# Query blocks two at a time from DRAM, and five and four exponential buffers instead of four and three, in a pre-LayerNorm attention and gated MLP block

## The chip, the cores and the metric

One core of a Trainium2 chip runs the whole kernel in one launch. The metric is the device time of one execution in microseconds. Timed runs and a separately profiled execution are told apart throughout: durations of single instructions come from the profiled one.

## The reference

A transformer block on 2048 rows of 640 columns: attention with 32 heads of 20 columns each, then a gated product of two matrices of 1728 columns, both behind a layer normalisation without weights, both added to their input.

```
h  = x + A(_layernorm(x), A_wqkv, A_wo)
h2 = h + B(_layernorm(h), B_w_gate, B_w_up, B_w_down)

A: q, k, v = split(x @ wqkv)              # 32 heads of 20
   p = softmax(q k^T * 20 ** -0.5)
   return (p v) @ wo
B: return ((x @ w_gate) * (x @ w_up)) @ w_down
```

Inputs and output are bfloat16, x is 1 x 2048 x 640.

## The kernel before

**Layout.** The 32 heads stand in 8 groups of four. Within a group each head has a slot of 32 partitions, of which 20 hold its query or key columns and one a constant. Rows of queries come in four blocks of 512 (blocks 0 to 3), keys in 16 tiles of 128.

**Stages.** The attention is a stream of 679 stages. Stage i issues score products (line 737, emit_S) for three (even i) or two (odd i) units into the PSUM tile sc0 or sc1, a unit being 128 keys against up to 512 queries of one head. ScalarE then takes one exponential over the whole tile (line 745) and writes it to a buffer E: E0 of 1536 columns for even stages, E1 of 1024 for odd ones. EB = (4, 3) says how many buffers there are of each. In most odd stages and some even ones a further unit goes to VectorE, which makes its exponential from integer operations (di, dm, dt; lines 757 and 640 to 645).

**Attention products.** The products of E with the values (line 885, emit_AV) read E and add up in one PSUM bank. One round is up to four products of different heads, in the four column groups of the array. An E buffer is free when all rounds that read it have been issued.

**The planner.** The order of all instructions is made in Python while the kernel is built. It keeps clocks for TensorE, VectorE and ScalarE (estimates) and, between the scores of one stage and the next, fills TensorE with attention rounds and with pieces of jobs from a queue (fill_step): projections, output products, the MLP's products. Before stage i writes its buffer, free_of(("e", i - 2 * EB[i % 2])) sees to it that the buffer's earlier readers have been issued. Where they haven't, it issues rounds at once, the last of them also with fewer than four heads. Where there is nothing to fill with, idle products are issued (idle_products).

**Queries and keys.** Most projections are written to DRAM in a dense form (dense, line 377) and read back into slots (read_slots, line 400) by four transfers, one per slot. Keys have one tile kT for all 2048 rows. Queries have qa for blocks 0 to 2 and qb for block 3. Groups 0 to 3 of block 0 are made directly in slots, and job spill (line 1130) writes them to DRAM, where a second version of the attention, for sums out of range, would read them. The rows of the slots that transfers never touch are filled once at the start (line 200).

**Tails.** When the queries of a block (block 0) or of half a block (blocks 1 to 3) are normalised, a tail is queued: output product, layer normalisation, MLP (job_glu, job_y), store. The MLP's up and gate matrices come in seven pairs of 256 columns (fp 0 to 6; the last is narrower), 320 KB a matrix. Two buffers for each of up (wu) and gate (wg) are refilled in turn (load_w). When block 3's stages begin, load_res takes the space of qa (wres) for pairs RES0 = 3 to 6, which the tails behind it find there. The last half-tail (last_tail) starts with the kept pairs, then takes 0 and 1, and pair 2 from two E0 buffers.

**Queues.** All transfers are issued by SyncE, one queue in the program's order: a transfer that waits holds those behind it.

Of the kernel before, what the change touches and what calls it, by code (L numbers as in the profile page):

```python
# [10 lines left out]
BF16 = mybir.dt.bfloat16  # L11
# [7 lines left out]
P = 128  # L19
S = 2048  # L20
D = 640
H = 32
DH = 20
NT = S // P
KT = D // P
# [24 lines left out]
SPLIT_3 = 2  # L50
QA = 3 * QB
RES0 = 3
SM_SCALE = float(DH) ** -0.5
# [28 lines left out]
SLACK = 100  # L82
EB = (4, 3)
POOL_LN = 3500
# [4 lines left out]
def kernel(  # L89
# [51 lines left out]
    qa, qb, kT = [[x[:, g, :] for g in range(NG)] for x in (qa_all, qb_all, kT_all)]  # L141
    dense = [dram.tile([D, S], BF16, name=f"dense{m}", bufs=1) for m in range(2)]
# [39 lines left out]
    for m in (1, 0):  # L182
        src = pads[m]
        runs = [(kT_all, 0, GP, QB, S), (kT_all, GP, NG, 0, S)] if m else [(qa_all, 0, GP, QB, QA), (qa_all, GP, NG, 0, QA), (qb_all, 0, NG, 0, QB)]
# [178 lines left out]
    def job_dense(m, t, ch):  # L363
        yield ROUND * KT
        ps = bank()
        for c in range(KT):
            for k in range(0, P, SLOT):
                col = t * P + k
                nc.tensor.matmul(ps[k:k + SLOT, :], lhsT=wqk_half(c, col // HALF)[:, m, col % HALF:col % HALF + SLOT],  # L369
                                 rhs=lnT[:, c, ch * QB:(ch + 1) * QB], start=(c == 0), stop=(c == KT - 1))  # L370
            mm(ROUND)
            if c < KT - 1:
                yield None
        dn = dnp.tile([P, QB], BF16, name="dn")
        nc.vector.tensor_copy(dn[:], ps[:])
        ev(QB, held["slot"])
        nc.sync.dma_start(dense[m][t * P:(t + 1) * P, ch * QB:(ch + 1) * QB], dn[:])
        written[m, t, ch] = clk["dve"] + WRITE
        for it in slot_sets:
            if it["m"] == m and it["ch"] == ch and all((m, x, ch) in written for x in it["ts"]) and not it["on"]:  # L380
                later(3, lambda it=it: read_slots(it))
# [10 lines left out]
    def read_slots(it):  # L392
        if it["on"]:
            return
        it["on"] = True
        m, ch, (g0, g1) = it["m"], it["ch"], it["gs"]
        dst, c0 = (kT_all, ch * QB) if m else (qb_all, 0) if ch == NB - 1 else (qa_all, ch * QB)
        src = dense[m][:, ch * QB:(ch + 1) * QB].rearrange("(g j e) n -> j e g n", j=HPG, e=DH)
        for j in range(HPG):
            nc.sync.dma_start(dst[SLOT * j:SLOT * j + DH, g0:g1, c0:c0 + QB], src[j, :, g0:g1, :])  # L400
        for key in it["keys"]:
            done.add(key)
            ready[key] = max([clk["pe"]] + [written[m, t, ch] for t in it["ts"]]) + READ

    def ensure_qk(key):
        if key not in done and key in slot_of:
            it = slot_of[key]
            for t in it["ts"]:
                ensure(("dn", it["m"], t, it["ch"]))
            read_slots(it)  # L410
        ensure(key)
        clk["pe"] = max(clk["pe"], ready.get(key, 0))
# [60 lines left out]
    LAST_B, LAST_T = NB - 1, [2, 3]  # L473
    first_b = [next(k for k, u in enumerate(us) if all(PASS[segs[v[0]][0]][0] == LAST_B for v in us[k:])) for us in (a_units, d_units)]
    pos = {"a": 0, "d": 0}
# [652 lines left out]
    def spill(j):  # L1128
        src = dense[0][:, 0:QB].rearrange("(g j e) n -> j e g n", j=HPG, e=DH)
        nc.sync.dma_start(src[j, :, 0:G1, :], qa_all[SLOT * j:SLOT * j + DH, 0:G1, 0:QB])  # L1130

# [102 lines left out]
    def load_res():  # L1234
        old = qkp.tile([P, NG, QA], BF16, name="wres", tag="qa")
        for k, fp in enumerate(range(RES0, FP)):
            late["res"][fp] = [w_tile(src, fp, old[:, 2 * k + m, :])
                               for m, src in enumerate((B_w_up, B_w_gate))]

# [133 lines left out]
    def last_tail():  # L1373
# [101 lines left out]

    seen = {"t": 0, "last": False}
    i = 0
    clk["dve"] = max(clk["dve"], clk["pe"])
    while pos["a"] < len(a_units) or pos["d"] < len(d_units):
        now["i"] = i  # L1480
        emit_S(i)
        if i == 0:
            first_rest()
        if not seen["last"] and pos["a"] >= first_b[0] and pos["d"] >= first_b[1]:
            for j in range(HPG):
                ensure(("spill", j))
            load_res()
            seen["last"] = True
        dve_fill(clk["pe"] + AHEAD)
# [119 lines left out]
```

## Time and profile before

| | us |
|---|---|
| timed runs, median of three | 870.62 (863.52 to 872.59) |
| profiled execution, whole | 861.78 |
| its span, first to last instruction | 860.0 |
| first exponential starts | 14.45 |
| last exponential ends | 810.42 |
| granted TensorE clock, mean | 0.999 of full speed |

The page splits the span by engine and by line. PE is TensorE's products, PEld its weight loads, DVE VectorE, ACT ScalarE, POOL GpSimd, SPq SyncE's queue. A row of a group has the line, engine, operation, what it writes and reads, and the count; then busy time, the mean of one in ns, and the engine's idle time just ahead of it with what ended that.

### The profile page before, as it was taken

How to read it: one execution, taken by the hardware profiler on the slowest of the kernel's cores; microseconds unless marked ns; L12 is line 12 of the kernel's file. 1: busy time of each engine (PE TensorE's matmuls, PEld its weight loads, DVE VectorE, ACT ScalarE, POOL GpSimd, SP SyncE). 2: the span in 40 equal slices, each digit the busy share in tenths (PEclk: the TensorE clock that was granted, in tenths of full speed). 3: DMA queues.
4: the chain of work that ended last, by engine and by line, in shares of the span. 5: the costliest groups of instructions: out<-in, count | busy, mean ns of one | idle time of the engine just before them, and what ended most of it. 6: DMA issues, size and time to landing. Idle time of an engine off the chain costs nothing.

```text
span 860.0 us, 34381 instructions
## 1 busy us (share of the span) xinstructions
PE 820.1 (95%) x15264; PEld 406.0 (47%) x15264; DVE 701.9 (82%) x1384; ACT 798.8 (93%) x711; POOL 191.3 (22%) x259
## 2 busy tenths in 40 slices
PE   8999999999999999999999999999999999999996
PEld 6334343332334334455444555555454556555775
DVE  7766788889779989888888889888988888889742
ACT  7999999999999999999999999999999999999621
POOL 2220000445214223212240323121411141114000
PEclk9999999999999999999999999999999999999999
DMA  6211201443330323101314031413510311031310
GB/s 187 70 50 45 68 16 61 105 119 70 66 95 16 118 76 78 40 15 34 100 41 130 24 100 34 116 39 107 124 40 15 107 32 33 9 100 47 88 46 19
DMA packets 94159, 57.62 MB, mean 67 GB/s; under 512 B 24436, under 2 KB 91892, under 8 KB 94004
## 3 DMA queue, kind: packets, MB, share of 16 engines
q1 hardware_dynamic: 94004, 55.36, 24.1%
q8 instruction: 121, 1.98, 0.9%
q14 instruction: 34, 0.28, 0.1%
HBM read 46.94 MB, written 8.16 MB: 64 GB/s over the span
## 4 chain that ended last, share of the span: by engine, by line
PE 49%; DVE 22%; ACT 21%; issue 5%; DMA 1%; POOL 1%; SPq 0%; DVEq 0%; ACTq 0%; POOLq 0%
ACT E L745 21%; PE sc L737 12%; PE acc L885 10%; PE mi L295 9%; PE mi L1251 8%; DVE di L757 7%; DVE di L645 3%; PE mi L369 3%; DVE dm L640 2%; DVE dt L642 2%; PE f L295 2%; PE f L1251 2%; DVE st L220 1%; PE mi L737 1%; DVE hh L1283 1%
## 5 line engine op out<-in xcount | busy, mean ns | idle before, releaser
L745 ACT ACTIVATE E<-sc 128x1536 bf16<-128x1536 f32 (+1 forms) x679 | 781.6, 1263 | 15.6 <-PE mi L737 7.0
L757 DVE TENSOR_SCALAR di<-mi 128x512 int16<-128x512 f32 x350 | 237.7, 684 | 62.1 <-PE mi L737 59.4
L885 PE MATMUL acc<-E,vx 128*32 128x256 bf16 (+1 forms) x2532 | 223.2, 314 | 1.6 <-DVE asb L915 1.4
L737 PE MATMUL sc<-qa,kT 21*128 21x256 bf16 (+1 forms) x1800 | 204.6, 319 | 12.2 <-ACT E L745 9.8
L782 POOL TENSOR_TENSOR rr<-rr,powers 128x8 f32<-128x8 f32 (+1 forms) x44 | 96.5, 2194 | 406.3 <-DMA rr<-sums 406.2
L737 PEld LDWEIGHTS <-kT 21*128 21x128 bf16 x3072 | 85.8, 91 | 212.3 <-issue 201.4
L885 PEld LDWEIGHTS <-vx 128*32 128x32 bf16 x3612 | 81.7, 95 | 106.4 <-issue 99.2
L645 DVE TENSOR_TENSOR di<-di,dm 128x1024 bf16<-128x1024 bf16 x175 | 122.6, 700 | 4.6
L737 PE MATMUL mi<-qa,kT 21*128 21x256 bf16 (+1 forms) x376 | 98.1, 311 | 2.9 <-DVE di L757 1.8
L640 DVE TENSOR_SCALAR dm<-di 128x1024 int16<-128x1024 int16 x175 | 77.2, 441 | 3.5
L885 PE MATMUL acc<-di,vx 128*32 128x256 bf16 (+1 forms) x540 | 76.6, 308 | 0.8 <-DVE di L645 0.5
L642 DVE TENSOR_SCALAR dt<-di 128x1024 int16<-128x1024 int16 x175 | 77.4, 442 | 0.0
L885 PE MATMUL acc<-dt,vx 128*32 128x256 bf16 (+1 forms) x540 | 77.1, 310 | 0.0
L737 PE MATMUL sc<-qb,kT 21*128 21x256 bf16 (+1 forms) x732 | 66.8, 288 | 2.9 <-ACT E L745 2.4
L295 PE MATMUL mi<-wd,hh 128*32 128x320 bf16 x1344 | 62.2, 300 | 1.0 <-DVE di L757 0.6
L1251 PE MATMUL mi<-ln2T,wg 128*32 128x256 bf16 (+1 forms) x1170 | 55.6, 298 | 1.4 <-DVE di L757 0.6
L1251 PE MATMUL mi<-ln2T,wu 128*32 128x256 bf16 (+1 forms) x1170 | 54.6, 298 | 1.2 <-DVE di L757 0.5
L295 PEld LDWEIGHTS <-hh 128*32 128x32 bf16 (+1 forms) x1456 | 45.6, 96 | 17.9 <-issue 8.1
L1251 PEld LDWEIGHTS <-wu 128*32 128x32 bf16 (+1 forms) x1190 | 32.4, 96 | 13.8 <-issue 9.6
L1251 PEld LDWEIGHTS <-wg 128*32 128x32 bf16 (+1 forms) x1190 | 32.6, 96 | 13.2 <-issue 9.2
L295 PE MATMUL mi<-kT,ident 128*32 128x512 bf16 x516 | 36.2, 382 | 1.3 <-DVE di L757 1.0
L266 DVE CAST u<-mi 128x512 bf16<-128x512 f32 x49 | 33.4, 683 | 4.8 <-PE mi L1251 4.8
(139 smaller groups left out, 788.4 us busy)
## 6 DMA issues: line engine op xcount, KB each, us to landing
wu<-in_B_w_up_dram SPq DMA_DIRECT2D x29, 320.0 KB
wg<-in_B_w_gate_dram SPq DMA_DIRECT2D x29, 320.0 KB
dense<-dn SPq DMA_DIRECT2D x36, 128.0 KB
bc<-scr SPq DMA_DIRECT2D x64, 64.0 KB
bc<-scr SPq DMA_DIRECT2D x112, 32.0 KB
xr<-in_A_x_dram SPq DMA_DIRECT2D x16, 160.0 KB
out_dram<-xr SPq DMA_DIRECT2D x14, 160.0 KB
wd<-in_B_w_down_dram SPq DMA_DIRECT2D x13, 160.0 KB
```

Source lines behind the costliest of these rows:

```text
L266: nc.vector.tensor_copy(dst, src)
L295: nc.tensor.matmul(out[k:k + w, :], lhsT=lhsT[:, k:k + w], rhs=rhs, **flags)
L369: nc.tensor.matmul(ps[k:k + SLOT, :], lhsT=wqk_half(c, col // HALF)[:, m, col % HALF:col % HALF + SLOT], rhs=lnT[:, c, ch * QB:(ch + 1) * ...
L640: nc.vector.tensor_scalar(m16[:, 0:n], s16, M_MASK, M_BITS, ALU.bitwise_and, ALU.bitwise_or)
L642: nc.vector.tensor_scalar(t16[:, 0:n], s16, E_MASK, E_BITS, ALU.bitwise_and, ALU.bitwise_or)
L645: nc.vector.tensor_tensor(sb[:, 0:n], sb[:, 0:n], mb[:, 0:n], ALU.mult)
L737: nc.tensor.matmul(dst[:, h * w:(h + 1) * w], lhsT=kT[g][SLOT * j:SLOT * j + VS, (kt + h) * P:(kt + h + 1) * P], rhs=q_of(g, b, c0, w)[SLO ...
L745: nc.scalar.activation(e[:, 0:n], sc[:, 0:n], ACT.Exp, bias=EXP_BIAS, scale=SM_SCALE)
L757: nc.vector.tensor_scalar(t[:, k * BANK:(k + 1) * BANK], sd[:], EXP_A, 0.0, ALU.mult, ALU.max)
L782: nc.gpsimd.tensor_tensor(ri, r16, powers[:, 1:2].to_broadcast([P, n]), ALU.pow)
L885: nc.tensor.matmul(acc["t"][SLOT * j:SLOT * (j + 1), 0:w], lhsT=vx[kt][:, VS * h:VS * h + SLOT], rhs=e, start=(j not in acc["new"]), stop= ...
L1251: nc.tensor.matmul(ps[r0 + x:r0 + x + d, col:col + n], lhsT=wt[:, c, f0 + x:f0 + x + d], rhs=st["ln2T"][:, c, c0:c0 + n], start=(c == 0), ...
```

## The change

The tile qa of three blocks and qb of one become two tiles q0 and q1 of one block each, used in turn. Blocks 0 and 1 are read as before. Block 2 is asked for when block 1's stages begin and all four spills and its dense pieces have been issued, block 3 when block 2's begin (next_q). The memory that this leaves goes to a fifth E0 and a fourth E1 buffer and to a tile of three places (spare) for weights. load_res keeps pairs 4 to 6 instead of 3 to 6: three matrices in spare, three in q0. The last half-tail brings pairs 2 and 3 into four E0 buffers.

```diff
-QA = 3 * QB
-RES0 = 3
+RES0 = 4
-EB = (4, 3)
+EB = (5, 4)
-    qa_all = qkp.tile([P, NG, QA], BF16, name="qa")
-    qb_all = qkp.tile([P, NG, QB], BF16, name="qb")
+    q_all = [qkp.tile([P, NG, QB], BF16, name=f"q{k}") for k in range(2)]
+    spare = qkp.tile([P, 3, KT * FPW], BF16, name="spare")
-        runs = [...] if m else [(qa_all, 0, GP, QB, QA), (qa_all, GP, NG, 0, QA), (qb_all, 0, NG, 0, QB)]
+        runs = [...] if m else [(q_all[0], GP, NG, 0, QB), (q_all[1], 0, NG, 0, QB)]
-        return qb[g][:, c0:c0 + w] if b == NB - 1 else qa[g][:, b * QB + c0:b * QB + c0 + w]
+        return q_all[b % 2][:, g, c0:c0 + w]
-            if it["m"] == m and it["ch"] == ch and all(...) and not it["on"]:
+            if it["m"] == m and it["ch"] == ch and all(...) and not it["on"] and (m or ch < 2):
+    def spilled():
+        for j in range(HPG):
+            ensure(("spill", j))
+    def next_q(b):
+        it = slot_of["q", b, 0]
+        if not all((0, t, b) in written for t in it["ts"]) or not all(("spill", j) in done for j in range(HPG)):
+            later(1, lambda: next_q(b))
+        elif not it["on"]:
+            read_slots(it)
...
     def load_res():
-        old = qkp.tile([P, NG, QA], BF16, name="wres", tag="qa")
+        old = qkp.tile([P, NG * QB], BF16, name="wres", tag="q0")
+        places = [spare[:, k, :] for k in range(3)] + [old[:, k * n:(k + 1) * n] for k in range(3)]
...
-        st["w", 2] = [w_tile(src, 2, e_tile(0)) for src in (B_w_up, B_w_gate)]
+        for fp in range(2, RES0):
+            st["w", fp] = [w_tile(src, fp, e_tile(0)) for src in (B_w_up, B_w_gate)]
...
-            for j in range(HPG):
-                ensure(("spill", j))
-            load_res()
+            if seen["block"] < LAST_B:
+                next_q(seen["block"] + 1)
+            else:
+                load_res()
```

ScalarE's order stays as it is, row for row. TensorE's has the same number of products, in another order. On TensorE before, ahead of the scores of stage 239 (sc_6157 is that stage's PSUM tile; L332 is fill work, a transposition):

```order
L332 MATMUL mi<-ident,ln_6059 128x128
L885 LDWEIGHTS vx_126
L885 MATMUL acc<-E_6009,vx_126 32x512
L885 LDWEIGHTS vx_128
L885 MATMUL acc<-E_6101,vx_128 32x512
L885 LDWEIGHTS vx_128
L885 MATMUL acc<-E_6101,vx_128 32x512
L737 LDWEIGHTS kT
L737 MATMUL sc_6157<-qa,kT 128x512
```

After, ahead of the scores of the same stage (sc_6097):

```order
L750 MATMUL mi<-q_114,kT 128x512
L898 LDWEIGHTS vx_132
L898 MATMUL acc<-dt,vx_132 32x512
L898 LDWEIGHTS vx_134
L898 MATMUL acc<-dt,vx_134 32x512
L898 LDWEIGHTS vx_126
L898 MATMUL acc<-E_5934,vx_126 32x512
L898 LDWEIGHTS vx_128
L898 MATMUL acc<-E_6033,vx_128 32x512
L750 LDWEIGHTS kT
L750 MATMUL sc_6097<-q_114,kT 128x512
```

Before, a round of three heads, with the buffer E_6009 that stage 239 needs, is the last thing ahead of the scores; after, it is a round of four.

On SyncE before, where block 3's stages begin (wres are the kept matrices, wu and wg the streamed ones):

```order
L793 DMA bc_14953<-scr 32x256 x4
L1224 DMA wres<-in_B_w_up_dram 128x5x256
L1224 DMA wres<-in_B_w_gate_dram 128x5x256
L1224 DMA wres<-in_B_w_up_dram 128x5x256
L1224 DMA wres<-in_B_w_gate_dram 128x5x256
L1224 DMA wres<-in_B_w_up_dram 128x5x256
L1224 DMA wres<-in_B_w_gate_dram 128x5x256
L1224 DMA wres<-in_B_w_up_dram 128x5x192
L1224 DMA wres<-in_B_w_gate_dram 128x5x192
L787 DMA scr<-rr 128x8
```

And after:

```order
L1237 DMA spare<-in_B_w_up_dram 128x5x256
L1237 DMA spare<-in_B_w_gate_dram 128x5x256
L1237 DMA spare<-in_B_w_up_dram 128x5x256
L1237 DMA wres<-in_B_w_gate_dram 128x5x256
L1237 DMA wres<-in_B_w_up_dram 128x5x192
L1237 DMA wres<-in_B_w_gate_dram 128x5x192
L800 DMA scr<-rr 128x8
L806 DMA bc_15180<-scr 32x256 x4
L1237 DMA wu<-in_B_w_up_dram 128x5x256
L1237 DMA wg<-in_B_w_gate_dram 128x5x256
L1237 DMA wu<-in_B_w_up_dram 128x5x256
L1237 DMA wg<-in_B_w_gate_dram 128x5x256
```

Eight kept matrices became six, and behind the next normalisation step two streamed pairs follow where there was one.

More of the change, by code (lines that the diff above doesn't have):

```diff
@@ L379, in job_dense @@
         for it in slot_sets:
-            if it["m"] == m and it["ch"] == ch and all((m, x, ch) in written for x in it["ts"]) and not it["on"]:
+            if it["m"] == m and it["ch"] == ch and all((m, x, ch) in written for x in it["ts"]) and not it["on"] and (m or ch < 2):
                 later(3, lambda it=it: read_slots(it))
@@ L409, in ensure_qk @@
                 ensure(("dn", it["m"], t, it["ch"]))
+            if key[0] == "q" and key[1] == 2:
+                spilled()
             read_slots(it)
@@ L473 @@
     LAST_B, LAST_T = NB - 1, [2, 3]
-    first_b = [next(k for k, u in enumerate(us) if all(PASS[segs[v[0]][0]][0] == LAST_B for v in us[k:])) for us in (a_units, d_units)]
+    first_of = [[next(k for k, u in enumerate(us) if all(PASS[segs[v[0]][0]][0] >= b for v in us[k:])) for us in (a_units, d_units)] for b in range(NB)]
+    first_b = first_of[LAST_B]
     pos = {"a": 0, "d": 0}
@@ L1474, in idle_products @@
             mm(ROUND)
-    seen = {"t": 0, "last": False}
+    seen = {"t": 0, "block": 0}
     i = 0
```

16 lines of the change are left out of this document (8 added, 8 removed).

## The prediction

> **What bounds the kernel now.** I read the page first, then the waits, then ScalarE's and TensorE's timelines around the waits, and last the end of the span. In the page, columns of a group's row are busy us, mean ns of one, and the idle time just ahead with what ended it.
>
> ```profile
> span 860.0 us, 34381 instructions
> PE 820.1 (95%) x15264; PEld 406.0 (47%) x15264; DVE 701.9 (82%) x1384; ACT 798.8 (93%) x711; POOL 191.3 (22%) x259
> ...
> PE 49%; DVE 22%; ACT 21%; issue 5%; DMA 1%; POOL 1%; SPq 0%; DVEq 0%; ACTq 0%; POOLq 0%
> ...
> L745 ACT ACTIVATE E<-sc 128x1536 bf16<-128x1536 f32 (+1 forms) x679 | 781.6, 1263 | 15.6 <-PE mi L737 7.0
> ```
>
> Two engines run almost through: TensorE and ScalarE. DMA is 1% of the chain that ended last. ScalarE's 679 exponentials (one per stage) are a stream that is hardly ever idle. The view of waits shows how the two hold each other up (total us, times, longest):
>
> ```profile
> PE sc L737 <- ACT E L745: 12.2, 48, 0.7
> ACT E L745 <- PE mi L737: 7.0, 21, 0.7
> ACT E L745 <- PE sc L737: 5.6, 16, 1.2
> ```
>
> TensorE waits 12.2 us for ScalarE, ScalarE 12.6 us for TensorE's scores. Neither is slack for the other: the kernel is a handshake between two nearly full engines. The stream itself, from ScalarE's timeline (start, length, what, how many, idle before) and the group by shape:
>
> ```profile
> 14.45 22.13 ACT L745 ACTIVATE E<-sc 128x1536 bf16<-128x1536 f32 x19 [1.21 <-PE sc L737]
> ...
> 99.33 30.99 ACT L745 ACTIVATE E<-sc 128x1536 bf16<-128x1536 f32 x27
> ...
> 796.27 14.15 ACT L745 ACTIVATE E<-sc 128x1024 bf16<-128x1024 f32 x12 [0.16 <-PE mi L737]
> ...
> L745 ACT ACTIVATE E<-sc 128x1536 bf16<-128x1536 f32 x340 | 501.5, 1475 | 5.1 <-PE sc L737 3.3 <-PE mi L737 1.1
> ```
>
> It runs from 14.45 to 796.27 + 14.15 = 810.42 us: 795.97 us for 339.5 pairs of a wide and a narrow exponential, 2.345 us a pair. Where it is well fed, 27 of them (14 wide, 13 narrow) take 30.99 us; less one wide of 1.475 that is (30.99 - 1.475) / 13 = 2.270 a pair. So the stream is 339.5 x 0.075 = 25 us longer than it would be if it were fed like that throughout. 12.6 us of it are the visible waits; the rest are exponentials that start late enough to lose their overlap with the one ahead. ScalarE's work is untouched by the change (the same exponentials in the same order), so no more than about 25 us can be won in the stream, and only what late scores cost.
>
> **The change part by part.** *More exponential buffers.* Before the scores of stage i are issued, the planner asks that the buffer of that stage is free (free_of); if it isn't, it places rounds of attention products (L885) there and then, ahead of the scores, even with fewer than four heads in a round. With 4 and 3 buffers this happens in stage 239 and in stage 461. TensorE's and ScalarE's timeline at the two:
>
> ```profile
> 290.36 0.40 PE L885 MATMUL acc<-E,vx 128*32 128x512 bf16 x3
> 290.68 0.60 PE L737 MATMUL sc<-qa,kT 21*128 21x512 bf16 x5
> 291.17 2.37 ACT L745 ACTIVATE E<-sc 128x1024 bf16<-128x1024 f32 x2 [0.67 <-PE sc L737]
> ```
> ```profile
> 550.98 0.95 PE L1251 MATMUL mi<-ln2T,wg 128*32 128x256 bf16 x28
> 551.74 0.27 PE L885 MATMUL acc<-E,vx 128*32 128x256 bf16 x1
> ...
> 552.09 0.27 PE L885 MATMUL acc<-E,vx 128*32 128x256 bf16 x1
> ...
> 552.30 0.28 PE L737 MATMUL sc<-qa,kT 21*128 21x256 bf16 x2
> ...
> 552.79 2.37 ACT L745 ACTIVATE E<-sc 128x1024 bf16<-128x1024 f32 x2 [0.72 <-PE mi L737]
> ```
>
> In the first a round of three heads stands between the fill work and the scores, in the second four rounds do, and ScalarE is idle 0.67 and 0.72 us. To count them I ran the planner of both files and noted each stage in which a buffer had to be freed first: 83 of 679 before, 26 after. Then I matched the 679 exponentials of the trace in turn with the stages and took, for each, how much later it ended than the usual 1.343 (wide) or 0.916 us (narrow) after the one ahead. The 83 stages are late by 10.2 us together, 0.123 each; the other 595 (the first has none ahead) by 18.5 us, 0.031 each. What a forced round costs is the difference, 0.092 us, so 7.6 us in all. 57 such stages go: 57 x 0.092 = **-5.2 us**. From below, 0: a round taken from here is issued elsewhere, where it may make other scores late. From above, 12.6 us, all visible waits. I take 5.2, as it is measured on the stages concerned.
>
> *Fuller rounds.* The attention products are the same 3612, but rounds with fewer than four heads fall from 144 to 98, which is 10 rounds of 512 columns in all. A round of four costs, from 16 products of four rounds:
>
> ```profile
> 608.27 1.05 PE L295 MATMUL mi<-kT,ident 128*32 128x512 bf16 x16
> ...
> 288.68 0.40 PE L885 MATMUL acc<-E,vx 128*32 128x512 bf16 x4
> ```
>
> (1.05 - 0.40) / 3 = 0.22 us each, 2.2 us of TensorE. It is the room in which the fill work of the next term could go, so I don't count it a second time; alone it would be the whole gain if TensorE were the limit (a rival below).
>
> *What is left over behind the stream.* A shorter stream gives the planner fewer gaps to put weight products into. In the program, 240 products of the up and gate matrices of block 3's first half-tail stand behind the last scores before, 340 after. The row of the rest that runs alone, and what follows it:
>
> ```profile
> 812.47 4.00 PE L1251 MATMUL mi<-ln2T,wres 128*32 128x256 bf16 x140
> ...
> 816.39 0.31 PE L1383 MATMUL f<-xr,ident 128*128 128x320 bf16 x1
> ```
>
> 4.00 / 140 = 0.029 us each, and nothing hides them: they end where the last tail's first product starts. 100 x 0.029 = **+2.9 us**. From below 0, if the real stream leaves gaps that the planner doesn't see.
>
> *Queries read per block.* The twenty transfers stay twenty, of the same size; only blocks 2 and 3 are read later, into a buffer that the block before the last has left. The issue of the last block's four:
>
> ```profile
> 198.99 1.56 SPq L400 DMA_DIRECT2D qb<-dense  x4
> ```
>
> After, the planner asks for block 2 when block 1 starts and for block 3 when block 2 starts, some 170 stages of 1.17 us ahead of their use (795.97 / 679 each): 195 us for transfers that are issued in 1.56. The wait for the last score product of the old block stands in SyncE's queue, and behind it the next step of a normalisation; the scores concerned are issued stages earlier, so 0. If the cover were gone it would be one transfer, the 4 us of the row below. Four fill transfers fewer at the start lie ahead of no first use: 0. The spill of block 0 stands where it stood, but now the read of block 2 must follow it; both are in one queue: 0.
>
> *One pair of weights fewer kept.* The fourth pair (up and gate, 320 KB each) is now streamed in three tails of the last 167 stages, and brought into two more exponential buffers for the last one. SyncE's issue and TensorE's first use of a streamed pair, one landing from the chain of waits, and the queue's longest wait for a buffer:
>
> ```profile
> 450.89 0.92 SPq L1224 DMA_DIRECT2D wu<-in_B_w_up_dram  x1
> ...
> 458.81 1.06 PE L1251 MATMUL mi<-ln2T,wu 128*32 128x256 bf16 x32
> ...
> 611.56 4.05 DMA wres<-in_B_w_up_dram
> ...
> SPq L1224 <- PE sc L737: 24.1, 14, 3.9
> ```
>
> Two buffers give 458.81 - 450.89 = 7.9 us from issue to use; a landing among seven others took 4.05. So 0, up to 4.05 for each tail if that cover goes. In the last tail:
>
> ```profile
> 831.57 0.39 SPq L1224 DMA_DIRECT2D E<-in_B_w_up_dram  x1
> 832.06 0.54 SPq L1224 DMA_DIRECT2D E<-in_B_w_gate_dram  x1
> ...
> 843.17 2.35 PE L1251 MATMUL f<-ln2T,E 128*128 128x256 bf16 x20
> ```
> ```profile
> 832.00:834.00 2.00, 2.00 (x21) 1.79 (x20) 0.69 (x1) 0.40 (x2) 0.00 (x0) 1.00 0.82 221
> 834.00:836.00 2.00, 2.00 (x21) 1.80 (x19) 0.69 (x1) 0.45 (x1) 0.00 (x0) 1.00 0.65 185
> 836.00:838.00 2.00, 2.00 (x24) 1.66 (x23) 0.69 (x1) 0.59 (x1) 0.00 (x0) 1.00 0.00 0
> ```
>
> (busy of PE, PEld, DVE, ACT, POOL, clock, DMA share, GB/s.) The pair is in by 836 us. Four pieces at 200 GB/s are in by about 840 (640 KB more, 3.3 us); the third pair is used from 841.0 (one pair of 20 products, 2.2 us, ahead of 843.17), the fourth at 843.17. So 0, with 3 us to spare.
>
> **The sum.** The profiled execution took 861.78 us: its span of 860.0 and 1.78 around it. 861.78 - 5.2 + 2.9 = 859.5, that is -0.27%. The median of the three timed runs is 870.62, which is 1.0% above the profiled one; on that scale 868.3.
>
> **The rivals.** *All of ScalarE's waits go.* If the forced rounds also push the stages behind them, removing them frees more than their own lateness. The 12.6 us of visible waits gone and the 2.9 us paid: 852.1, or 860.8 by the median (-1.1%). For it: the two largest waits above (0.67, 0.72) stand right behind forced rounds. Against it: of the other large ones most stand in stages without any, and late scores there come from fill work. [...]
>
> *TensorE is the limit, and nothing much moves.* It is 95% busy; then only the 2.2 us of fuller rounds count: 859.6, 868.4 by the median, or 870.6 where even these are given back. [...]
>
> *The streamed pair is late (slower).* In the three tails and the last one TensorE reaches the fourth pair before it has landed, since its load waits in SyncE's queue behind normalisation steps that themselves wait. Place: the first up product of the fourth pair. Price: up to 4.05 us in each of four places, half of it 8.1, and with the 2.9 us behind the stream and no gain within it +11.0: 872.8, or 881.7 by the median. It decides where less than 4.05 us lie between issue and use; 7.9 us of the row speak against it, the 3.9 us that the queue was seen to wait for it.
>
> *The change doesn't do what it says.* The planner could be held by VectorE's buffers instead, which stay as they are. Speaking against it: of the rounds forced before, 107 of 123 were for exponential buffers, and 34 are left. It would give 870.6.
>
> **How the numbers follow.** A measurement of this kernel tells about 1% from no change, as the three runs lie between 863.52 and 872.59. The forecast, 868 us: 0.36, its own range from 863 (-7.6 us, nothing paid behind) to 874 (nothing gained, 2.9 paid). TensorE the limit, or no effect: 0.14, also within 1%. All waits gone: 0.28, faster by over 1%, which holds anything from there to all of the 25 us. The streamed pair late, or another step of the new order late: 0.22, slower by over 1%. That makes 0.28, 0.50, 0.22. The range reaches from 856 (a little beyond all waits gone) to 879 (most of the late pair's price).
>
> **What would show it.** Right: ScalarE's waits on L737's successor fall from 12.6 towards 9 us, the last exponential ends near 805 instead of 810.4, and the products that run alone before the last tail grow by 2.9 us. The forced rounds at stage 239 and 461 are gone and ScalarE is not idle there. Wrong: the last exponential ends at 810 or later, waits of TensorE on weight, query or spare transfers of over 1 us, or the last pair's first use behind 844 by more than the shift of the whole end.

## The result and the profile after

The changed kernel takes 874.38 us in the median of 11 runs (872.69 to 878.67), the kernel before 863.71 in 11 runs beside it (861.15 to 872.59): a ratio of 1.0116, 95% interval 1.0089 to 1.0142. The profiled execution took 874.38 us, its span is 872.6 (860.0 before); the two profiles lie 12.6 us apart, the medians 10.7. The page of the changed kernel, with the rows that answer to those of before:

```profile
span 872.6 us, 34370 instructions
...
PE 826.1 (95%) x15264; PEld 406.9 (47%) x15264; DVE 703.4 (81%) x1384; ACT 798.9 (92%) x711; POOL 192.5 (22%) x259
...
PEclk9999999999999899999999999999999999998999
...
L758 ACT ACTIVATE E<-sc 128x1536 bf16<-128x1536 f32 (+1 forms) x679 | 781.7, 1274 | 25.5 <-PE mi L750 11.1
```

ScalarE's work is the same (781.7 us, 781.6 before), but it now stands idle for 25.5 us ahead of exponentials instead of 15.6, and TensorE's clock is under full speed in two slices of the stream where before it was nowhere. The view of waits of the same kernel (us in all, times, longest):

```profile
PE sc L750 <- ACT E L758: 14.6, 61, 0.6
ACT E L758 <- PE mi L750: 11.1, 23, 1.4
ACT E L758 <- PE sc L750: 11.1, 20, 3.0
...
PE mi L1265 <- DVE ln2T L265: 4.0, 4, 2.1
```

ScalarE's waits for scores did not fall from 12.6 to about 9 us; they rose to 22.2. The last row has grown most: TensorE's first up product waits for ln2T, the normalised and transposed rows that VectorE copies out of PSUM. The same row in the kernel before:

```profile
PE mi L1251 <- DVE ln2T L266: 0.5, 2, 0.3
```

The end of the stream and what runs alone behind it, from TensorE's and ScalarE's timelines:

```profile
806.52 13.78 ACT L758 ACTIVATE E<-sc 128x1024 bf16<-128x1024 f32 x12 [0.24 <-PE mi L750]
...
822.81 3.46 PE L1265 MATMUL mi<-ln2T,spare 128*32 128x256 bf16 x120
826.08 3.06 PE L1265 MATMUL mi<-ln2T,wres 128*32 128x256 bf16 x100
829.08 0.31 PE L1397 MATMUL f<-xr,ident 128*128 128x320 bf16 x1
```

The last exponential ends at 806.52 + 13.78 = 820.3 us instead of 810.4, and what follows it takes 52.3 us instead of 49.6. So 9.9 us are lost in the stream and 2.7 behind it.

Where in the stream? Matched stage by stage, the changed kernel is ahead by 2.9 us at stage 240, the way the forecast's first term has it. Then it loses 4.6 us in stages 241 to 260, 1.7 in 581 to 600 and 3.9 in 661 to 678. This is the last of these places, on all three engines:

```profile
796.00 0.44 PE L331 MATMUL mi<-ident,ln 128*128 128x128 bf16 x5
...
797.40 0.69 DVE L658 TENSOR_TENSOR di<-di,dm 128x1024 bf16<-128x1024 bf16 x1
798.01 0.42 DVE L928 COPY asb<-acc 128x256 f32<-128x256 f32 x1
798.34 0.48 DVE L265 COPY ln2T<-mi 128x640 bf16<-128x640 bf16 x1
...
798.88 1.69 PE L1265 MATMUL mi<-ln2T,wu 128*32 128x256 bf16 x28 [2.11 <-DVE ln2T L265]
...
801.15 1.45 ACT L758 ACTIVATE E<-sc 128x1536 bf16<-128x1536 f32 x1 [3.03 <-PE sc L750]
```

TensorE has transposed the rows by 796.44, but VectorE has other work queued ahead of the copy and makes it at 798.34. The first up product waits 2.11 us, everything behind it on TensorE waits too, the next scores among it, and ScalarE is idle for 3.03 us. The windows of the same place (busy us of PE, PEld, DVE, ACT, POOL in each 2 us, granted clock, DMA share, GB/s):

```profile
796.00:798.00 2.00, 0.76 (x9) 0.47 (x9) 1.97 (x4) 2.00 (x2) 0.71 (x2) 0.96 0.00 0
798.00:800.00 2.00, 1.12 (x24) 0.95 (x27) 1.49 (x5) 0.12 (x1) 0.00 (x0) 0.50 0.01 2
800.00:802.00 2.00, 2.00 (x38) 0.98 (x34) 0.00 (x0) 0.85 (x1) 0.00 (x0) 0.50 0.07 10
```

Behind the thin stretch the granted clock is 0.50, here for 6.83 us (797.82 to 804.65), and once more for 6.83 us from 292.65, behind a hand-over of rows near 289 us. At that place VectorE is late because one operation that takes 0.43 us elsewhere took 1.45, while GpSimd scaled an accumulator (timelines of VectorE and GpSimd):

```profile
287.09 1.45 DVE L653 TENSOR_SCALAR dm<-di 128x1024 int16<-128x1024 int16 x1
...
286.98 1.26 POOL L810 TENSOR_TENSOR part<-asb,bc 128x512 bf16<-128x512 f32 x1
```

GpSimd's operation starts 0.11 us earlier, and VectorE's, of 1.45 us, ends 0.3 us after it.

### The profile page after: what moved, and what is told of

Its sections match the earlier page's. It is cut to its first block, busy times and chain, and to the rows that moved or that the text cites. A ratio compares the mean times of both kernels' runs of the same rounds, so it can differ in the third digit from the quotient of the medians.

```text
span 872.6 us, 34370 instructions
## 1 busy us (share of the span) xinstructions
PE 826.1 (95%) x15264; PEld 406.9 (47%) x15264; DVE 703.4 (81%) x1384; ACT 798.9 (92%) x711; POOL 192.5 (22%) x259
## 5 line engine op out<-in xcount | busy, mean ns | idle before, releaser
L758 ACT ACTIVATE E<-sc 128x1536 bf16<-128x1536 f32 (+1 forms) x679 | 781.7, 1274 | 25.5 <-PE mi L750 11.1
L750 PE MATMUL sc<-q,kT 21*128 21x256 bf16 (+1 forms) x2532 | 272.8, 312 | 17.8 <-ACT E L758 14.6
L898 PE MATMUL acc<-E,vx 128*32 128x256 bf16 (+1 forms) x2532 | 217.3, 316 | 0.1
L750 PE MATMUL mi<-q,kT 21*128 21x256 bf16 (+1 forms) x540 | 134.6, 305 | 3.6 <-DVE di L770 1.7
L898 PE MATMUL acc<-di,vx 128*32 128x256 bf16 (+1 forms) x540 | 74.3, 310 | 0.2 <-DVE di L658 0.2
L1265 PE MATMUL mi<-ln2T,wu 128*32 128x256 bf16 (+1 forms) x1290 | 61.4, 304 | 6.6 <-DVE ln2T L265 4.0
L1265 PE MATMUL mi<-ln2T,wg 128*32 128x256 bf16 (+1 forms) x1290 | 59.8, 296 | 0.7 <-DVE di L770 0.4
L1265 PEld LDWEIGHTS <-wu 128*32 128x32 bf16 (+1 forms) x1310 | 36.4, 98 | 20.8 <-issue 16.1
L1265 PEld LDWEIGHTS <-wg 128*32 128x32 bf16 (+1 forms) x1310 | 36.0, 96 | 11.8 <-issue 7.6
L810 POOL TENSOR_TENSOR part<-asb,bc 128x256 bf16<-128x256 f32 (+1 forms) x23 | 21.4, 933 | 69.0 <-DMA bc<-scr 54.0
```

The source lines that it names most:

```text
L750: nc.tensor.matmul(dst[:, h * w:(h + 1) * w], lhsT=kT[g][SLOT * j:SLOT * j + VS, (kt + h) * P:(kt + h + 1) * P], rhs=q_of(g, b, c0, w)[SLO ...
L758: nc.scalar.activation(e[:, 0:n], sc[:, 0:n], ACT.Exp, bias=EXP_BIAS, scale=SM_SCALE)
L810: nc.gpsimd.tensor_tensor(On[b % 2][g][:, c0:c0 + w], asb[:, 0:w], bc[:, 0:w], ALU.mult)
L898: nc.tensor.matmul(acc["t"][SLOT * j:SLOT * (j + 1), 0:w], lhsT=vx[kt][:, VS * h:VS * h + SLOT], rhs=e, start=(j not in acc["new"]), stop= ...
L1265: nc.tensor.matmul(ps[r0 + x:r0 + x + d, col:col + n], lhsT=wt[:, c, f0 + x:f0 + x + d], rhs=st["ln2T"][:, c, c0:c0 + n], start=(c == 0), ...
```

## The experiments

Theory A was formed from this: the new order brings late hand-overs from VectorE to TensorE, and behind some of them TensorE's clock is halved. Its rivals: B, the query reads or the streamed fourth pair cost; C, the waits alone cost and the half clock is hidden; D, any order other than the one before loses; F, the forecast's two terms price an order after all. Ratios are to the kernel before, timed on the same chip in the same rounds.

| kernel | ratio, 95% interval | stream in the profile, us | of it at half clock | TensorE's waits for VectorE |
|---|---|---|---|---|
| before | 1 | 796.0 | 0 | 14.6 |
| changed | 1.0116 (1.0089 to 1.0142) | 806.0 | 13.7 | 19.3 |
| q_res4 | 1.0023 (0.9998 to 1.0048) | 803.2 | 17.1 | 13.5 |
| after_warm | 1.0069 (1.0043 to 1.0095) | 801.3 | 0 | 18.3 |
| after_split | 1.0051 (1.0025 to 1.0076) | 803.0 | 10.2 | 18.8 |
| after_act | 1.0022 (0.9998 to 1.0046) | 799.0 | 3.4 | 16.5 |
| after_gate | 1.0138 (1.0071 to 1.0206) | 806.2 | 10.2 | 19.1 |
| before_late | 1.0023 (0.9993 to 1.0052) | 801.1 | 6.8 | 16.0 |
| before_split | 0.9967 (0.9941 to 0.9994) | 798.6 | 6.8 | 12.1 |
| b44 | 1.0129 (1.0055 to 1.0203) | 809.6 | 17.1 | 19.1 |
| b53 | 1.0241 (1.0180 to 1.0303) | 825.1 | 34.1 | 26.6 |
| before_ease10 | 1.0033 (1.0008 to 1.0057) | 802.1 | 10.2 | 16.0 |
| before_avlow6 | 1.0041 (1.0012 to 1.0070) | 804.8 | 13.7 | 15.5 |
| after_ahead300 | 0.9918 (0.9887 to 0.9949) | 798.3 | 10.2 | 14.0 |
| after_ahead400 | 1.0033 (1.0006 to 1.0060) | 799.0 | 17.1 | 15.0 |
| after_ahead500 | 1.0065 (1.0035 to 1.0095) | 803.9 | 20.5 | 16.5 |
| before_ahead300 | 1.0191 (1.0147 to 1.0235) | 819.8 | 20.5 | 21.6 |
| after_ahead300_split | 0.9900 (0.9857 to 0.9942) | 792.8 | 10.2 | 9.6 |

The stream runs from the start of the first to the end of the last exponential. The last column sums all rows of the view of waits in which TensorE waits for VectorE. The three columns of the profile are one execution each; how much of it ran at half clock differs from run to run.

### Queries and weights without the buffers: q_res4

```diff
-EB = (5, 4)
+EB = (4, 3)
```

> The changed kernel with 4 and 3 exponential buffers as before: queries of two blocks, reads per block and one more streamed weight pair stay, and every engine's computation stands in the order of the kernel before. Theory A (the loss sits where the new order hands normalised rows over while VectorE is late, and TensorE's clock halves): the order is the old one, so the time is that of before, within 0.4%, and no halved clock before 850 us. Theory B (the reads of queries or the streamed fourth pair cost): 4 us or more above before, with TensorE waiting for weight or query transfers.

1.0023: no difference that its interval shows, and in its profile TensorE waits 0.5 us at most for any transfer. So B falls, and with it the forecast's rival of the late streamed pair. The edit also showed that the order hangs on the buffers alone: every engine's computation stands as in the kernel before, up to the turn of the weight pairs in the last half-tail. Its profile fell on three stretches of half clock, which the expectation excluded, and so measures their price in an order that is otherwise the same. ScalarE's timeline of q_res4 around the third, its windows, and ScalarE's timeline in the kernel before at the same stages:

```profile
744.68 6.91 ACT L758 ACTIVATE E<-sc 128x1024 bf16<-128x1024 f32 x6 [0.20 <-PE mi L750]
752.44 2.37 ACT L758 ACTIVATE E<-sc 128x1024 bf16<-128x1024 f32 x2 [0.85 <-PE mi L750]
756.11 1.02 ACT L758 ACTIVATE E<-sc 128x1024 bf16<-128x1024 f32 x1 [1.30 <-PE mi L750]
757.37 8.44 ACT L758 ACTIVATE E<-sc 128x1536 bf16<-128x1536 f32 x7 [0.23 <-PE sc L750]
766.10 9.15 ACT L758 ACTIVATE E<-sc 128x1024 bf16<-128x1024 f32 x8 [0.30 <-PE mi L750]
```
```profile
748.00:750.00 2.00, 1.96 (x38) 0.97 (x26) 1.12 (x5) 2.00 (x2) 0.20 (x2) 1.00 0.00 0
750.00:752.00 2.00, 2.00 (x22) 1.29 (x22) 1.72 (x4) 1.59 (x2) 1.07 (x3) 0.50 0.01 4
```
```profile
739.87 6.91 ACT L745 ACTIVATE E<-sc 128x1024 bf16<-128x1024 f32 x6 [0.20 <-PE mi L737]
747.15 11.46 ACT L745 ACTIVATE E<-sc 128x1024 bf16<-128x1024 f32 x10 [0.37 <-PE mi L737]
758.90 10.07 ACT L745 ACTIVATE E<-sc 128x1024 bf16<-128x1024 f32 x9 [0.30 <-PE mi L737]
```

Both run six exponentials in 6.91 us. Then the clock is halved for 6.83 us in the one and not in the other, and what was 744.68 - 739.87 = 4.81 us behind is 766.10 - 758.90 = 7.20 behind: 2.4 us for one such stretch. The other two, at 463 and 620 us, cost 2.2 and 2.3. The half clock is not hidden: C falls as a whole account.

The runs say the same without the profile. Each run lists its granted clock. Over the 31 runs of the kernel before that stand beside this one, the time follows 862.25 us + 0.33 for each us at half clock (correlation 0.94): 861.98 at a clock of 1.000, 871.70 at 0.984, that is 2 x 0.016 x 871.7 = 28 us at half (the profiles of the kernel before and of the changed one record clocks of 1.0 and 0.5 alone). The ten runs of q_res4 follow 862.1 + 0.43: at equal clock the two kernels take the same time.

### TensorE kept busy in the same order: after_warm

```diff
+    by_cols(ps[:, 0:QB].bitcast(F32), ident[:], kT[0][:, 0:HW], start=True, stop=True)   # six times, ahead of one tile's transposes
+    by_cols(ps[:], ident[:], kT[0][:, 0:QB], start=True, stop=True)   # five and eight times, ahead of two first up products
```

> The changed kernel, same order, with products on data that are overwritten put where TensorE stood idle: six of 256 columns ahead of the transposes near 289 us, five and eight of 512 columns ahead of the first up product near 710 and 799 us (0.6, 1.1 and 1.8 us of work, nearly all inside waits of 0.3, 1.2 and 2.1 us). Theory A: the clock stays full at 292.65 and 797.82, and the last exponential ends 3 to 6 us earlier than 820.3, so the time falls by 0.3 to 0.7% against the changed kernel (869 to 872 on the scale of 874.4). Theory C (the waits alone cost, the halved clock is hidden behind ScalarE): time unchanged or up to 1 us longer.

1.0069 against 1.0116: 0.47% or 4 us less, as theory A said, though 76 more products are issued. The clock is full at all three places, and over the ten runs it is 0.998 in the median (0.990 in the changed kernel); this window is from where it was 0.50 in the changed kernel:

```profile
798.00:800.00 2.00, 2.00 (x64) 1.16 (x56) 1.24 (x3) 1.98 (x2) 0.68 (x1) 1.00 0.10 17
```

So about 4 us of the loss are the half clock, and the rest is in the order itself: three runs at a clock of 1.000 took 870.0 to 870.4 us, 8 us more than the kernel before at that clock (862.25). With a full clock throughout, this stream is still 801.3 - 796.0 = 5.3 us longer than before. The two stages behind the first up products, 591 and 664, are late by 1.5 and 1.8 us of that.

### GpSimd's product in pieces: after_split, before_split

```diff
-nc.gpsimd.tensor_tensor(On[b % 2][g][:, c0:c0 + w], asb[:, 0:w], bc[:, 0:w], ALU.mult)
+for x in range(0, w, P):
+    nc.gpsimd.tensor_tensor(On[b % 2][g][:, c0 + x:c0 + x + P], asb[:, x:x + P], bc[:, x:x + P], ALU.mult)
```

> The changed kernel with GpSimd's product of a normalisation (128x512 or 128x256) issued in pieces of 128 columns; order and results as they were on all other engines. Near 287 us one VectorE operation that usually takes 0.43 us took 1.45, while that product ran. Theory A with GpSimd as its cause: VectorE's longest operation of that line falls to 0.9 us or less, the hand-over near 289 us comes some 0.5 to 1 us earlier, at least one of the two stretches of half clock is gone, and the time falls by 2 to 6 us. If GpSimd's product isn't what holds VectorE, or pieces hold it as long: same time, both stretches of half clock remain.

1.0051, some 5.6 us less than the changed kernel. VectorE's and GpSimd's timelines at the place of the 1.45 us:

```profile
289.13 0.63 DVE L653 TENSOR_SCALAR dm<-di 128x1024 int16<-128x1024 int16 x1
...
289.02 2.00 POOL L811 TENSOR_TENSOR part<-asb,bc 128x128 bf16<-128x128 f32 x4
```

VectorE's operation beside the four pieces (2.00 us in all) took 0.63 us instead of 1.45, and the half clock near 292 us is gone; the one at 795 is not, since the 2 us wait for ln2T there has another cause. A new one of 3.41 us came at 204.56, behind a VectorE operation that took 1.60 us beside two of GpSimd's fills of the tile wo, which this edit leaves whole.

> The kernel before, in its own order, with GpSimd's product of a normalisation issued in pieces of 128 columns. In the changed kernel this took 0.65% off. Theory A (VectorE's late operations behind GpSimd's product make late hand-overs in any order): 1 to 4 us less than before, a ratio of 0.995 to 0.999, and no VectorE operation of these lines over 0.9 us beside that product. If it mattered in the changed kernel only by where a halved clock fell: no change, 1.000.

0.9967 (0.9941 to 0.9994): the edit helps the old order too, 2.8 us. It is a version faster than both kernels, with one line changed. One of these VectorE operations still took 1.08 us, from the last piece of a product on into what GpSimd did next, where the expectation had 0.9 at most. It also changes how after_split is to be read: with the pieces in both kernels the ratio is 1.0051 / 0.9967 = 1.0084, so of the 1.16% only about 0.3 points belong to GpSimd's products in the new order, and each of the two ratios is known to about 0.26 points.

### One late hand-over made, two taken away: before_late, after_act, after_gate

```diff
-            evac(eng, dst, ps[:].rearrange("p (c k) -> p c k", k=P))
+            for k in range(times):   # 5 for the last tile of block 3's first half-tail
+                evac(eng, dst, ps[:].rearrange("p (c k) -> p c k", k=P))
```

> The kernel before, with VectorE's copy of the last transposed rows of block 3's first half-tail made five times instead of once (four more of 0.48 us, 1.9 us, near 786 us), so that TensorE's first up product waits there. Theory A: the 3.4 us around it fall under about 0.55 busy, the clock is halved for 6.83 us, and the end comes 4 to 6 us later than before. Theory C: the end comes at most 1.9 us later, whatever the clock does.

A miss for theory A. TensorE waited (its timeline and windows):

```profile
792.75 1.17 PE L1252 MATMUL mi<-ln2T,wu 128*32 128x256 bf16 x36 [1.40 <-DVE ln2T L266]
```
```profile
788.00:790.00 2.00, 1.50 (x28) 0.87 (x22) 2.00 (x5) 2.00 (x2) 0.22 (x1) 1.00 0.04 2
790.00:792.00 2.00, 1.35 (x32) 0.67 (x28) 1.90 (x5) 1.72 (x3) 0.00 (x0) 1.00 0.00 0
```

but the clock stayed full. Stages 660 to 678 lost 1.47 us, the wait and nothing more; the rest of the 5.1 us in this profile came at two stretches of half clock elsewhere. TensorE was busy for 59% of the 3.41 us from 790.14, less than the 63% ahead of the half clock at 797.82 in the changed kernel, so this share alone does not decide. The 0.55 of the expectation was the author's estimate; no run shows a limit there. Here the late hand-over passed on its own length, without a half clock behind it.

For after_act, ScalarE makes two copies, on top of after_split:

```diff
-                yield from job_T(st["l", t], st["ln2T"][:, :, t * P:(t + 1) * P])
+                on_act = (key, t) in (((2, 2), 3), ((3, 0), 1))
+                yield from job_T(st["l", t], st["ln2T"][:, :, t * P:(t + 1) * P], "act" if on_act else "dve")
```

> The changed kernel with GpSimd's product in pieces (1.005 of before), in the same order, and at the two hand-overs near 710 and 799 us ScalarE copies the last transposed rows instead of VectorE (two copies of about 0.6 us). Theory A: TensorE's waits of 1.2 and 2.1 us for the rows fall under 1 us together, the clock isn't halved near 798, and with 1.2 us added to ScalarE the time falls by 1 to 4 us against the pieces alone (1.001 to 1.004 of before). Rival (VectorE is late for what follows too, so another wait takes the place): 1.005 or more.

1.0022 against 1.0051 with the pieces alone; the intervals overlap, the place agrees in part. In the profile stages 660 to 678 take 2.0 us less than in after_split. But the clock was still halved there, at 793.00 for 3.41 us (6.83 in after_split), which theory A excluded, and the waits for ScalarE's copies are above its 1 us. The remaining waits:

```profile
PE mi L1267 <- ACT ln2T L263: 1.6, 2, 1.1
PE mi L1267 <- DVE ln2T L265: 0.7, 2, 0.4
```

The two places wait 1.6 us instead of 3.3. Together, with pieces and copies, the loss of 1.16% against the kernel before falls to 0.22% in the changed kernel's own order. Against the kernel before with the pieces, 1.0022 / 0.9967 = 1.0055 are left.

For after_gate, the planner holds the first up product back:

```diff
+        until = clk["pe"] + {(2, 2): 1500, (3, 0): 1500}.get(key, 0)
+        while clk["pe"] < until and not forced["on"]:
+            yield WAIT
```

> The changed kernel, in which the planner holds the first up product of two half-tails (block 2's second, block 3's first) for 1.5 us behind the transposes and puts attention or idle products there; 340 weight products stand behind the last scores, as in the changed kernel. Theory A: TensorE's waits of 1.2 and 2.1 us for the transposed rows fall under 0.5 in all, the clock isn't halved near 798, and the time falls by 3 to 6 us (a ratio to before of 1.005 to 1.008). Rival (TensorE's work is the limit, and what is held back is missed later): 1.010 to 1.014, as the changed kernel.

1.0138: the waits for ln2T fell to 0.7 us in all, as intended, but the time did not. The hold shifts all that follows into yet another order, which has its own half clock at 706.6 and 754.4 us. What removes a wait by re-planning is not an experiment on that wait alone.

### Do the forecast's terms price an order? b44, b53, before_ease10, before_avlow6

```diff
-EB = (5, 4)
+EB = (4, 4)   # b44; (5, 3) in b53
```

> The changed kernel with 4 and 4 exponential buffers: one narrow buffer more than before, no wide one; another order again. In the program 38 stages have forced rounds (83 before, 26 with the whole change) and 220 weight products stand behind the last scores (240 before, 340 with the whole change). Theory F (the forecast's two terms price an order: 0.092 us for each such stage, 0.029 us for each product behind): 45 x 0.092 + 20 x 0.029 = 4.7 us less than before, a ratio of about 0.995. Theory D (the terms price nothing; an order that isn't the one before loses by its own late hand-overs, whichever buffer is added): 1.003 to 1.012.

> The changed kernel with 5 and 3 exponential buffers: one wide buffer more than before, no narrow one. 87 stages with forced rounds (83 before), 140 weight products behind the last scores (240 before). Theory F: 4 x 0.092 - 100 x 0.029 = 2.5 us less than before, a ratio of about 0.997, and the stretch behind the last exponential 2.9 us shorter. Theory D: 1.003 to 1.012, with a stream of exponentials longer than before by more than what is saved behind it.

1.0129 and 1.0241 where the terms give 0.995 and 0.997. In b53 the term behind the stream holds (47.5 us behind the last exponential, 2.1 less), and the stream is 29 us longer. Its page and waits:

```profile
PEclk9999999997999999999979999999999989999999
...
L758 ACT ACTIVATE E<-sc 128x1536 bf16<-128x1536 f32 (+1 forms) x679 | 783.5, 1261 | 42.8 <-PE mi L750 24.7
```

ScalarE is idle for 42.8 us ahead of exponentials, TensorE waits 26.6 us for VectorE, and 34 us ran at half clock. In b44 the term behind the stream fails too: with 220 products behind instead of 240 this stretch is 52.6 us instead of 49.6. What makes its stream longer was not taken apart. The two neighbours of the old order:

```diff
-EASE, HURRY = 0, 100
+EASE, HURRY = 10, 100   # before_ease10
-AVLOW = 8
+AVLOW = 6   # before_avlow6, alone
```

> The kernel before with one number of its planner moved by a little: fill work may run 10 ns longer into the time before the next scores. Same buffers, queries and weights; another order (1,980 lines of TensorE's differ). In the program 79 stages with forced rounds (83 before), 240 products behind (as before), and the planner's own clock ends the last exponential at 784.6 us (783.5 before). Theory F: within 0.1% of before (0.37 us less by its terms). Theory D (the order before is one that happened to suit, and its neighbours lose without any change of buffers): 1.004 to 1.015.

> The kernel before with another number of its planner moved: attention rounds go ahead of fill work from seven waiting products instead of nine. Same buffers; another order (1,260 lines of TensorE's differ). 85 stages with forced rounds (83 before), 240 products behind, the planner's last exponential at 784.6 us (783.5). Theory F: within 0.1% of before. Theory D: 1.004 to 1.015.

1.0033 and 1.0041, both slower beyond their intervals, with nothing in their counts to say so (the planner's clock had 1.1 us of the 2.9 and 3.5). Theory D holds to this extent: the counts that were forecast with are blind to at least 0.4% between orders.

### Another order with the change: after_ahead300, 400, 500 and before_ahead300

```diff
-AHEAD = 700
+AHEAD = 300   # or 400, 500: how far ahead of TensorE's clock VectorE's side work is placed, ns
```

> The changed kernel with VectorE's side work placed at most 300 ns ahead of TensorE's clock instead of 700; another order. 20 stages with forced rounds (26 in the changed kernel, 83 before), 220 products behind (340, 240), the planner's last exponential at 779.3 us (779.6, 783.5). Theory F: 63 x 0.092 + 20 x 0.029 = 6.4 us less than before, 0.993. Theory D: it spreads as the others, 1.003 to 1.015, with the real last exponential 36 us or more behind the planner's (27 before, 41 in the changed kernel).

0.9918 (0.9887 to 0.9949): faster than the kernel before by 0.8%, where F says 0.993 and D 1.003 or more. In its view of waits this is all that is left of the waits for ln2T:

```profile
PE mi L1265 <- DVE ln2T L265: 0.5, 2, 0.3
```

> The kernel before, with its own buffers, queries and weights, and VectorE's side work placed at most 300 ns ahead. 88 stages with forced rounds, 100 products behind, the planner's last exponential at 793.3 us (783.5 before), three hand-overs of 1.00 to 1.20 us. If the gain at 300 ns came from the placing alone: 0.990 to 0.997. If it needs the buffers (both theories): the planner's 9.8 us more less 140 x 0.029 = 4.1 us saved behind, 1.005 to 1.012.

1.0191: the placing alone, without the buffers, loses. The planner's own clock said so here (793.3 us against 783.5); 3.5 us of the profile are one wait of TensorE for a streamed weight, wu.

> The changed kernel with VectorE's side work placed at most 400 ns ahead. Its planner's last exponential (779.4 us), forced stages (21) and most hand-overs (0.67 us at most) are those of 300 ns, but the copy of block 3's first half-tail ends 1.71 us after its first product starts, as in the changed kernel, and 340 products stand behind (220 with 300 ns). Theory A: a wait of about 2 us for the rows near 795 us is back, and with 120 x 0.029 = 3.5 us more behind the stream the time is 4 to 8 us above the kernel with 300 ns, 0.997 to 1.002 of before. If that hand-over doesn't matter: only the 3.5 us, 0.996 or less.

1.0033: the one late hand-over is back, 1.9 us long, and 340 products stand behind (53.8 us behind the last exponential against 50.5). The ratio is 0.0115, some 10 us, above the 300 ns order, more than either reading expected; the profile has two stretches of half clock, 17 us together, behind 698 us.

> The changed kernel with VectorE's side work placed at most 500 ns ahead instead of 700. In the planner's clock no copy of transposed rows ends more than 0.76 us after the first product that needs it starts (1.28 and 1.71 in the changed kernel, 0.67 at most with 300 ns, 1.23 and 1.00 before). 14 stages with forced rounds, 220 products behind, the planner's last exponential at 781.3 us (779.6 in the changed kernel, 779.3 with 300 ns, 783.5 before). Theory A (late hand-overs and what the clock makes of them cost; without them the forecast's terms hold): 0.992 to 0.998. Theory D (an order falls out well or badly, whatever these hand-overs are): as the other orders that were tried, 1.003 to 1.015.

1.0065: a miss for theory A as it was put, by the hand-overs of transposed rows, and for the forecast's terms, which give 6.9 us less than before. TensorE waits 1.0 us at most for these, but 1.90 us for another late hand-over from VectorE, the copy of a finished accumulator, and the clock is halved behind it (327.8 us, for 6.83). TensorE's timeline:

```profile
327.45 0.40 PE L898 MATMUL acc<-E,vx 128*32 128x256 bf16 x6 [1.90 <-DVE asb L928]
```

Stages 261 to 280 lose 4.7 us there against the fastest kernel. So a hand-over of another kind can do the same; the planner's figure for transposed rows tells only of one.

> The changed kernel with 300 ns (0.992 of before) and GpSimd's product of a normalisation in pieces of 128 columns, in the same order. If what the pieces save adds up: 0.985 to 0.990 (0.33% less in the kernel before, 0.65% in the changed one). If in an order without late hand-overs VectorE's late operations are covered: 0.990 to 0.994.

0.9900 (0.9857 to 0.9942), 856.66 us in the median beside 864.55: the fastest kernel here. Whether the pieces add to the 300 ns is not settled, as the two intervals overlap. Page and waits:

```profile
span 856.4 us, 34394 instructions
...
L758 ACT ACTIVATE E<-sc 128x1536 bf16<-128x1536 f32 (+1 forms) x679 | 779.5, 1274 | 14.5 <-PE mi L750 6.0
```
```profile
ACT E L758 <- PE mi L750: 6.0, 10, 1.4
ACT E L758 <- PE sc L750: 4.9, 10, 1.2
```

ScalarE waits 10.9 us for scores, 20 times (12.6 and 37 times before, 22.2 and 43 times in the changed kernel): the way that the extra buffers were forecast to act, though how much of it is theirs and how much the order's is not shown.

## Why the prediction was wrong

**What bounds the kernel** held: two nearly full engines in a handshake, and the losses that were found in the stream are TensorE late for ScalarE.

**The forced rounds** went as described: 83 stages became 26, ScalarE doesn't wait at stages 239 and 461, and by the same measure the stages with forced rounds are late by 4.3 us together instead of 10.2, 5.9 us less beside the 5.2 forecast. At stage 240 the kernel is 2.9 us ahead.

**The step that failed is the lower bound of this term**, "From below, 0: a round taken from here is issued elsewhere, where it may make other scores late". It let the first term come to nothing at worst and never to a loss: a change of order was taken as free. The other stages, 595 before and 652 after, are late by 34.4 us instead of 18.5. Small lateness, up to 0.3 us a stage, fell from 16.1 to 13.9 us, in which part of the forecast's gain shows; the stages over 0.3 us went from 26 with 12.6 us to 39 with 24.8. What the extra buffers buy in many small pieces is lost in a dozen large ones. About 4 us of these are the half clock and 3.3 us the stages behind the two waits for ln2T at 710 and 799 us (after_warm). The rest stays open: it is spread over the stream, and no run here took it apart.

The planner's clock could have told part of it: it lets the first up product start without asking for the last copy, and in its own reckoning this copy ends 1.28 and 1.71 us behind the last transposition at the two places, against 1.00 and 0.67 before. From the first product's start it is 0.85 and 1.39 us late, where before it was 0.86 and 1.03 us early. (The expectations above call the figures of the first kind lateness behind the first product; the planner has them from the last transposition.) The forecast counted forced rounds in the planner and not this.

**Behind the stream**: +2.9 us forecast, +2.7 measured; that it fits is in part luck, as b44 goes the other way. **Query reads and the streamed pair**: 0 forecast, and q_res4 shows no cost that its interval tells from none; in the changed kernel weights and queries make TensorE or its weight loads wait 0.2 us at most. **Fuller rounds** can't be read apart.

**The rivals**: none of the four happened as described. All waits gone and TensorE the limit fell with the waits that grew; the change did what it says; and the one that ended slower had the wrong mechanism, a late weight transfer. "Another step of the new order late" stood in its chance of 0.22 without a place or a price. Of the signs of being wrong, "the last exponential ends at 810 or later" was the one that came true.

**The scale** was off too: the forecast stood on three runs of the kernel before around 870.62 us, eleven give 863.71, on which the same forecast would be 861.4. That 874.38 lies between its 856 and 879 is luck of that scale.

That the buffers do not cost by themselves is shown by after_ahead300: one order with them is faster than the kernel before, 0.9918, and before_ahead300 shows that the placing alone does not do it, 1.0191. It is the best of four placings with the change, against four orders tried without. That this gain is the forecast's 0.993 is less than shown, since the orders differ in much else, and the same two terms miss in b44, b53, at 400 and at 500 ns.

## What to carry over

In a kernel whose order a planner sets, an edit of a buffer count is an edit of the whole order: price the hand-overs between engines in the new order, not only the stalls that go, and try a few neighbouring orders of both kernels before a gain or loss under 1% is put down to the edit. Isolate the part that leaves the order alone (here one line) and compare that first. Before comparing times, compare the granted clock of the runs.

## What the hardware showed that was not expected

**The clock is halved while TensorE is far from idle.** All stretches at half clock in the streams are 3.41, 6.83 or 10.24 us long, and within a run they start on one grid of 3.413 us (in the changed kernel 797.82 - 292.65 = 148 x 3.413). The streams of the 18 profiles, cut into windows on that grid, have 30 whole windows at full clock in which TensorE was at most 66% busy, and 23 of them were followed by a half clock (in the changed kernel those from 289.24, 66%, and 794.41, 63%, were, and the one from 709.08, 66%, was not); of the 4,124 busier ones, 17, such as the one ahead of 750 us in q_res4 (87%). The line at 66% was drawn afterwards; up to 75% it is 32 of 65. None of the 40 windows ahead of a half clock was idle (38% busy at least). In these 40 the transposes of rows took 9% of the time and the float32 products 5%, elsewhere 1% and 0.4%; no run tried either of them alone.

**One program's time differs by 1% with its time at half clock.** That is most of the spread of the kernel before, 861.98 to 871.70 us in 31 runs (correlation 0.94). That it hangs on where the grid falls in a run is a reading of the windows; no run moved the grid.

**GpSimd holds up VectorE by some products and not by others.** In the changed kernel's profile VectorE's operations of 0.42 us took up to 1.50 us beside its product of an accumulator; 44 of them that started inside its power of 8 or 16 columns (2.19 us in the mean by the profile) took 0.42 in the median and 0.45 at most. Over the 18 profiles 879 of 889 such took 0.50 or less, and the other ten ran on beside GpSimd's next product or fill.
